# Banded attention and a gated MLP on one core: the next pair's queries are scaled behind the scores of the pair at hand

## The chip, the cores and the metric

One core of one Trainium2 chip. The metric is the device time of one execution in microseconds (us); smaller is better. The times shown are from repeated executions of the whole program; one further execution was taken with the hardware profiler, and everything said of single instructions comes from that one. TensorE is called PE below, VectorE DVE, ScalarE ACT, GpSimd POOL; SP is the engine that issues the DMAs.

## What is computed

Attention over 4 batches of 8 heads (768 positions, 64 numbers a head), where a position sees the first 8 positions and the last 96, with a distance penalty per head; the heads' outputs side by side are the input of an MLP with the gate h * clip(h + 3, 0, 6) / 6.

```
scores = q @ k.T / sqrt(D) - slope[h] * dist      # kept where global or local, else -1e9
a = exp(scores - max); a = a / (sum(a) + 1e-9)
x = (a @ v) for all heads, as [B * S, H * D]      # [3072, 512]
h = x @ w_in                                      # [3072, 2048]
out = (h * clip(h + 3, 0, 6) / 6) @ w_out         # [3072, 512]
```

## The kernel before, in words

The 3072 rows are cut into 8 **blocks** of 384 rows (half a batch each). Of each block, attention is done in 4 **pairs** of heads, numbered through from 0 to 31; pair n belongs to block n // 4. A block's MLP runs in 16 steps f: `first` (L174) makes 128 of the 2048 hidden columns from the four pairs' outputs `xh`, `xl` in 12 matmuls, `gate` (L185 on ACT, L186 on DVE) makes `g`, `high` (L192, on POOL after the first blocks) and `rest` (L199, on DVE) split it in `gh` and `gl`, and `second` (L206) adds 9 matmuls to three accumulators.

Attention of one block is laid between the MLP steps of the block before it. The first nine pairs (0 to 8) are done another way, ahead of 150 us in the profile. Pairs 9 to 31 go through these steps:

- `scale` (L850, POOL): multiplies the queries of a pair in place, in the tile they were loaded into. The scores read them afterwards.
- `packed`: the scores, 24 small matmuls (L864, PE; the trace shows 48 records), then the mask and the row minimum (L893, DVE) and the exponentials with their sums (L897, ACT).
- `sum_up` (L907, L908, DVE) and `normalize` (L917, POOL, six instructions a pair, two for each tile t).
- `spread`: six 32x32 block transposes (L939, DVE) into `blocks`, which has one buffer, and behind the last of them four DMAs (L944, SP) to the DRAM tile `there`; then `fetch`, eight DMAs (L955, SP) from `there` into `weights`.
- `values` (L973, PE): weights times v. Its first four multiplications wait for the first four of the eight fetches, the fifth for the other four.

Loads: the keys and queries of pair n + 3 are loaded by `load_next` (L327, SP) into the room that pair n used, as soon as pair n's scores are done; there are three rooms (load_72, load_73, load_74).

What sets the order: `units[k]` is a list of calls that are made at the k-th yield of the generator which writes out the MLP steps (`halves` up to the end of block 1, `twos`, which takes two steps f together, from block 2 on). `in_order` ties the instructions of PE, SP and POOL to the order in which they are written; ACT and DVE are ordered by a scheduler when the program is built. Each engine runs its instructions in its order, so an instruction that waits holds up all behind it on its engine. In `halves`, step f's `first` is followed by one yield, then by `second` of step f - 1, then by another. `rest_of_third` fills the units for pairs 9 to 11 (and scales 12), `attention` those for pairs 12 to 31, four of a block at a time.

Of the kernel before, what the change touches and what calls it, by code (L numbers as in the profile page):

```python
# [20 lines left out]
NT = 3  # L21
# [44 lines left out]
class Kernel:  # L66
# [616 lines left out]
    def rest_of_third(self, x, slices):  # L683

        units = [[] for _ in range(2 * NF)]
        pairs = [Pair(self, n, x, False) for n in range(EARLY, 3 * NPAIR + 1)]
        pairs[0].scale()
        for p, (me, after) in enumerate(zip(pairs, pairs[1:])):
            at = units[3 * p + 1:]
            at[0] += [me.packed, lambda me=me: self.load_next(me.n, False)]  # L690
            at[1] += [me.sum_up] + [lambda t=t, me=me: me.normalize(t) for t in range(NT)]
            at[2] += [lambda t=t, me=me: me.spread(t) for t in range(NT)] + [me.fetch, after.scale]
        units[10].append(lambda: pairs[0].values("x"))
        units[2 * slices - 1].append(lambda: pairs[-3].values("x"))
        return units, pairs

    def attention(self, i, x, first):

        units = [[] for _ in range(2 * NF - 2)]
        pairs = [first]  # L700
        first.x = x
        for p in range(NPAIR):
            n = i * NPAIR + p
            me, after = pairs[p], Pair(self, n + 1, x, False) if n + 1 < len(self.blocks) * NPAIR else None
            pairs.append(after)
            at = units[6 * p:]
            at[0] += [me.packed, lambda me=me: self.load_next(me.n, False)]
            at[3] += [me.sum_up, lambda me=me: me.normalize(0), lambda me=me: me.normalize(1)]
            at[4] += [lambda me=me: me.normalize(2), lambda me=me: me.spread(0)]
            at[5] += [lambda me=me: me.spread(1), lambda me=me: me.spread(2), me.fetch]  # L710
            if after:
                at[4].append(after.scale)
            if p % 2 == 1:
                at[11] += [lambda me=pairs[p - 1]: me.values("x"), lambda me=me: me.values("s")]
        return units, pairs[NPAIR]
# [336 lines left out]
```

## Time and profile before

| what | us |
|---|---|
| three executions | 664.86, 662.81, 660.73 |
| their median | 662.81 |
| the profiled execution | 660.4 |
| its span, first to last instruction | 658.5 |
| PE busy in it | 640.4 |

The profiled execution took 1.9 us more than its span and lies 2.4 us below the median of the three. In the profile a row of the timeline gives the start in us from the span's start, the duration, the engine, the line, the operation, the tiles out<-in, the shapes, the count, and in brackets the idle time of the engine just before it and what ended that. A row with x48 joins 48 records. A queue's rows (SPq) show the time that the issue of a DMA takes, not its transfer.

### The profile page before, as it was taken

Reading aid. Unit: us, or ns where it says so; the run is one execution under the profiler, and the core shown is the slowest. Engines: PE = TensorE matmul, PEld = TensorE weight load, DVE = VectorE, ACT = ScalarE, POOL = GpSimd, SP = SyncE. Lnnn points to the kernel's source line nnn. Section 1 sums busy time; section 2 is a strip of 40 time slices with the busy share of each in tenths; the row PEclk is TensorE's granted clock in tenths of the full one; section 3 lists DMA queues with packets and bytes.
Section 4 is the critical chain, followed back from the end, with each engine's and each line's share of the span. In section 5 each row is a group of like instructions: output and inputs, shape, how many; then the busy total and the mean of one; then the engine's idle time right before and its main releaser. Section 6 shows DMA issues by size and latency. Waiting matters only on the chain.

```text
span 658.5 us, 13101 instructions
## 1 busy us (share of the span) xinstructions
PE 640.4 (97%) x4761; PEld 565.3 (86%) x4761; DVE 357.2 (54%) x1066; ACT 257.2 (39%) x706; POOL 166.8 (25%) x372
## 2 busy tenths in 40 slices
PE   9989999999799899999999999999999999999997
PEld 7778999997688788988898888988899888989985
DVE  5889999995544554255444454345552555422222
ACT  5897777775324232134313322132321433121111
POOL 4666000001431322033231243113230232202100
PEclk9999999999999999999999999999999999999999
DMA  7675545433564465326552365424653354300001
GB/s 275 183 231 198 193 151 159 136 122 113 134 189 156 122 166 166 96 83 161 173 158 76 115 173 167 125 92 132 179 144 93 102 143 121 103 30 21 1 0 54
DMA packets 47122, 86.23 MB, mean 131 GB/s; under 512 B 6504, under 2 KB 28872, under 8 KB 47048
## 3 DMA queue, kind: packets, MB, share of 16 engines
q1 hardware_dynamic: 46760, 85.03, 43.6%
q8 instruction: 40, 0.66, 0.4%
q14 instruction: 34, 0.28, 0.1%
q10 hardware_dynamic: 288, 0.26, 0.1%
HBM read 60.30 MB, written 24.97 MB: 129 GB/s over the span
## 4 chain that ended last, share of the span: by engine, by line
PE 87%; DVE 5%; ACT 3%; POOL 3%; issue 1%; DMA 1%; SPq 0%; POOLq 0%; ACTq 0%; DVEq 0%
PE hp L174 40%; PE acc L206 35%; PE xp L973 2%; ACT n L897 2%; PE sp L864 2%; PE sp L973 2%; POOL n L917 2%; PE sp L206 1%; PE xp L206 1%; PE tp L206 1%; DVE n L893 1%; DMA load<-pairs 1%; DVE blocks L939 1%; PE tp L864 1%; PE acc L973 1%
## 5 line engine op out<-in xcount | busy, mean ns | idle before, releaser
L185 ACT ACTIVATE g<-hp,small 128x384 f32<-128x384 f32 x127 | 73.5, 579 | 280.2 <-PE hp L174 187.0
L174 PE MATMUL hp<-xh,w1h 128*128 128x384 f32 x512 | 173.9, 340 | 0.5 <-ACT w1h L461 0.5
L174 PE MATMUL hp<-xh,w1l 128*128 128x384 f32 x512 | 172.4, 337 | 0.5 <-DVE w1l L450 0.5
L174 PE MATMUL hp<-xl,w1h 128*128 128x384 f32 x512 | 171.7, 335 | 0.0
L186 DVE SCALAR_TENSOR_TENSOR g<-g,hp 128x384 f32<-128x384 f32 x128 | 70.7, 553 | 128.0 <-ACT g L185 126.8
L192 POOL TENSOR_SCALAR gh<-g 128x384 fp32r<-128x384 f32 x104 | 53.3, 512 | 342.4 <-DVE g L186 316.3
L206 PE MATMUL acc<-w2h,gh 128*128 128x512 f32 x336 | 133.2, 397 | 0.0
L206 PE MATMUL acc<-w2h,gl 128*128 128x512 f32 x336 | 131.8, 392 | 0.0
L206 PE MATMUL acc<-w2l,gh 128*128 128x512 f32 x336 | 131.6, 392 | 0.0
L199 DVE TENSOR_TENSOR gl<-g,gh 128x384 fp32r<-128x384 f32 x128 | 71.5, 558 | 71.7 <-POOL gh L192 58.7
L897 ACT ACTIVATE n<-n,least 128x136 f32<-128x136 f32 (+2 forms) x192 | 79.5, 415 | 70.3 <-DVE least L893 69.5
L174 PEld LDWEIGHTS hp<-xh,w1h 128*128 128x128 f32 x512 | 96.1, 188 | 6.5 <-issue 3.1
L174 PEld LDWEIGHTS hp<-xl,w1h 128*128 128x128 f32 x512 | 96.1, 188 | 2.5
L174 PEld LDWEIGHTS hp<-xh,w1l 128*128 128x128 f32 x512 | 96.1, 188 | 1.1 <-DVE w1l L450 0.8
L917 POOL TENSOR_SCALAR n<-n,sums 128x136 f32<-128x136 f32 (+2 forms) x186 | 81.5, 455 | 45.9 <-DVE sums L908 27.2
L206 PEld LDWEIGHTS acc<-w2h,gh 128*128 128x128 f32 x336 | 63.1, 188 | 15.3 <-issue 3.1
L206 PEld LDWEIGHTS acc<-w2h,gl 128*128 128x128 f32 x336 | 63.0, 188 | 13.8 <-DVE gl L199 0.3
L206 PEld LDWEIGHTS acc<-w2l,gh 128*128 128x128 f32 x336 | 63.1, 188 | 11.5
L939 DVE STREAM_TRANSPOSE blocks<-n 128x256 f32<-128x256 f32 x138 | 51.0, 423 | 23.3 <-POOL n L917 22.7
L897 ACT ACTIVATION_READ_ACCUMULATOR n<-n,least 128x1 f32 x192 | 36.0, 187 | 0.0
L893 DVE CUSTOM_DVE_ANT_0 n<-sp,dl 128x136 f32<-128x136 f32 x60 | 17.7, 295 | 16.1 <-PE tp L864 16.1
L410 ACT ACTIVATE wz<-wst 128x512 f32<-128x512 f32 x32 | 21.4, 673 | 6.2 <-DVE w2l L450 2.8
(119 smaller groups left out, 647.3 us busy)
## 6 DMA issues: line engine op xcount, KB each, us to landing
there<-blocks SPq DMA_DIRECT2D x92, 192.0 KB
wst<-w SPq DMA_DIRECT2D x32, 512.0 KB
weights<-there SPq DMA_DIRECT2D x161, 96.0 KB
load<-pairs SPq DMA_DIRECT2D x31, 444.0 KB
load<-pairs SPq DMA_DIRECT2D x32, 384.0 KB
out<-o SPq DMA_DIRECT2D x23, 256.0 KB
weights<-there SPq DMA_DIRECT2D x23, 24.0 KB
there<-blocks SPq DMA_DIRECT2D x4, 72.0 KB
```

The source lines that it names most:

```text
L174: self.nc.tensor.matmul(hp, lhsT=self.w1(w, f)[:, kt, :], rhs=a[:, kt, :], start=(n == 0), stop=(n == 3 * NKT - 1))
L185: nc.scalar.activation(out=g, in_=hp, func=AF.Relu, bias=self.three, scale=1.0)
L186: nc.vector.scalar_tensor_tensor(out=g, in0=g, scalar=6.0, in1=hp, op0=ALU.min, op1=ALU.mult)
L192: self.nc.gpsimd.tensor_scalar(out=gh, in0=g, scalar1=1.0, scalar2=0.0, op0=ALU.mult, op1=ALU.add)
L199: self.nc.vector.tensor_tensor(out=gl, in0=g, in1=gh.bitcast(F32), op=ALU.subtract)
L206: self.nc.tensor.matmul(acc[tt], lhsT=a[:, tk], rhs=self.w2(w, f), start=(f == 0 and j == 0), stop=(f == NF - 1 and j == 2))
L410: self.nc.scalar.activation(out=self.z[i].bitcast(F32), in_=words[:, :, 1].bitcast(F32), func=AF.Abs)
L893: nc.vector.tensor_tensor_reduce(out=e[:, j, lo:end], in0=sp[j][:, lo:end], in1=d, op0=ALU.add, op1=ALU.min, scale=scale, scalar=3.0e38, a ...
L897: nc.scalar.activation(out=e[:, j, lo:end], in_=e[:, j, lo:end], func=AF.Exp, bias=self.least[:, i:i + 1], scale=-1.0, accum_out=self.sums ...
L917: nc.gpsimd.tensor_scalar(out=e[:, j, lo:end], in0=e[:, j, lo:end], scalar1=over, scalar2=0.0, op0=ALU.mult, op1=ALU.add)
L939: nc.vector.transpose(out=self.blocks[:, :, s, t].rearrange("p b j q -> p j b q"), in_=e[:, :, c:c + P].rearrange("p j (b q) -> p j b q", ...
L973: nc.tensor.matmul(xps[j * D:(j + 1) * D, t * P:(t + 1) * P], lhsT=vt[0:K, t, j * D:(j + 1) * D], rhs=self.part(t, j, c, K), start=(c == 0 ...
```

## The change

The call that scales the queries of pair n + 1 is moved from behind the normalization (and, for pairs 10 to 12, behind the transposes) of pair n to right behind the call that makes pair n's scores. Nothing is added or removed: 23 scalings before and after.

```
--- before.py
+++ after.py
@@ -687,9 +687,9 @@
-            at[0] += [me.packed, lambda me=me: self.load_next(me.n, False)]
+            at[0] += [me.packed, after.scale, lambda me=me: self.load_next(me.n, False)]
             at[1] += [me.sum_up] + [lambda t=t, me=me: me.normalize(t) for t in range(NT)]
-            at[2] += [lambda t=t, me=me: me.spread(t) for t in range(NT)] + [me.fetch, after.scale]
+            at[2] += [lambda t=t, me=me: me.spread(t) for t in range(NT)] + [me.fetch]
@@ -704,12 +704,10 @@
-            at[0] += [me.packed, lambda me=me: self.load_next(me.n, False)]
+            at[0] += [me.packed] + [a.scale for a in (after,) if a] + [lambda me=me: self.load_next(me.n, False)]
             at[3] += [me.sum_up, lambda me=me: me.normalize(0), lambda me=me: me.normalize(1)]
             at[4] += [lambda me=me: me.normalize(2), lambda me=me: me.spread(0)]
             at[5] += [lambda me=me: me.spread(1), lambda me=me: me.spread(2), me.fetch]
-            if after:
-                at[4].append(after.scale)
```

The changed file is two lines shorter, so lines below the change have numbers that are smaller by two (L850 is L848 there, L917 is L915, L939 is L937, L893 is L891).

First place: POOL, from the scaling of pair 9 (load_72) to the normalization of pair 11. The rooms go round, so load_73 is pair 10, load_74 pair 11, the second load_72 pair 12. Before:

```order
L850 TENSOR_SCALAR load_72<-load_72,over 128x384
L192 TENSOR_SCALAR gh<-g 128x384 x2
L917 TENSOR_SCALAR n<-n,sums 128x136 x6
L850 TENSOR_SCALAR load_73<-load_73,over 128x384
L192 TENSOR_SCALAR gh<-g 128x384
L917 TENSOR_SCALAR n<-n,sums 128x136 x6
L192 TENSOR_SCALAR gh<-g 128x384
L850 TENSOR_SCALAR load_74<-load_74,over 128x384
L192 TENSOR_SCALAR gh<-g 128x384
L917 TENSOR_SCALAR n<-n,sums 128x136 x6
L850 TENSOR_SCALAR load_72<-load_72,over 128x384
```

And of the change, on the same engine and from the same place:

```order
L848 TENSOR_SCALAR load_72<-load_72,over 128x384
L192 TENSOR_SCALAR gh<-g 128x384
L848 TENSOR_SCALAR load_73<-load_73,over 128x384
L192 TENSOR_SCALAR gh<-g 128x384
L915 TENSOR_SCALAR n<-n,sums 128x136 x6
L192 TENSOR_SCALAR gh<-g 128x384
L848 TENSOR_SCALAR load_74<-load_74,over 128x384
L915 TENSOR_SCALAR n<-n,sums 128x136 x6
L192 TENSOR_SCALAR gh<-g 128x384
L848 TENSOR_SCALAR load_72<-load_72,over 128x384
```

Each scaling stands ahead of the six normalizations that it stood behind, and pair 11's (load_74) ahead of one `gh` as well.

Second place: POOL, the first two pairs of block 3, 12 and 13, in `attention`; load_73 is pair 13 here, load_74 pair 14. Before:

```order
L192 TENSOR_SCALAR gh<-g 128x384 x5
L917 TENSOR_SCALAR n<-n,sums 128x136 x4
L192 TENSOR_SCALAR gh<-g 128x384 x2
L917 TENSOR_SCALAR n<-n,sums 128x136 x2
L850 TENSOR_SCALAR load_73<-load_73,over 128x384
L192 TENSOR_SCALAR gh<-g 128x384 x2
L917 TENSOR_SCALAR n<-n,sums 128x136 x6
L850 TENSOR_SCALAR load_74<-load_74,over 128x384
```

Of the change:

```order
L848 TENSOR_SCALAR load_73<-load_73,over 128x384
L915 TENSOR_SCALAR n<-n,sums 128x136 x4
L192 TENSOR_SCALAR gh<-g 128x384 x2
L915 TENSOR_SCALAR n<-n,sums 128x136 x2
L848 TENSOR_SCALAR load_74<-load_74,over 128x384
L192 TENSOR_SCALAR gh<-g 128x384 x2
L915 TENSOR_SCALAR n<-n,sums 128x136 x6
```

Pair 13's scaling is ahead of all six normalizations of pair 12 and of two `gh`; pair 14's stands ahead of pair 13's normalization and two `gh`.

Third place: DVE, which the scheduler orders, behind the scores of pair 10. Before:

```order
L907 TENSOR_SCALAR sums<-sums 128x6
L908 RECIPROCAL sums<-sums 128x6
L939 STREAM_TRANSPOSE blocks<-n 128x2x4x32 x6
L186 SCALAR_TENSOR_TENSOR g<-g,hp 128x384
L199 TENSOR_TENSOR gl<-g,gh 128x384
```

Of the change:

```order
L199 TENSOR_TENSOR gl<-g,gh 128x384
L905 TENSOR_SCALAR sums<-sums 128x6
L906 RECIPROCAL sums<-sums 128x6
L937 STREAM_TRANSPOSE blocks<-n 128x2x4x32 x2
L186 SCALAR_TENSOR_TENSOR g<-g,hp 128x384
L937 STREAM_TRANSPOSE blocks<-n 128x2x4x32 x4
L199 TENSOR_TENSOR gl<-g,gh 128x384
```

Here the `gl` that stood ahead of pair 10's six L893 now stands behind them, and the next step's `g` (L186) has moved in between the transposes. From there to the end of the banded part DVE's order is the same; PE, SP and ACT have the same order throughout it.

## The prediction

> **What bounds the kernel now.** I read the profile's page first (busy shares and PE's granted clock), then the list of PE's waits, then the timelines of PE, POOL, DVE and SP around those waits.
>
> ```profile
> PE 640.4 (97%) x4761; PEld 565.3 (86%) x4761; DVE 357.2 (54%) x1066; ACT 257.2 (39%) x706; POOL 166.8 (25%) x372
> PEclk9999999999999999999999999999999999999999
> ```
>
> PE is the bound, at full clock in every slice. It is idle for 658.5 - 640.4 = 18.1 us, and no change that leaves its instructions alone can bring more than that. Which part of it hangs on the scaling, PE's waits tell:
>
> ```profile
> PE acc L864 <- POOL load L850: 3.1, 1, 3.1
> PE sp L864 <- POOL load L850: 2.3, 2, 2.0
> PE acc L864 <- DVE g L186: 1.2, 1, 1.2
> ```
>
> The scores (L864) wait three times for the scaling, 5.4 us in all, and once, 1.2 us, for something put down to DVE. The places:
>
> ```profile
> 166.75 0.58 POOL L850 TENSOR_SCALAR load<-load,over 128x384 f32<-128x384 f32 x1
> 167.38 1.04 PE L864 MATMUL acc<-load 64*32 64x136 f32 x48 [1.24 <-DVE g L186]
> 171.98 2.15 POOL L917 TENSOR_SCALAR n<-n,sums 128x136 f32<-128x136 f32 x6 [3.96 <-DVE sums L908]
> 176.97 0.99 POOL L850 TENSOR_SCALAR load<-load,over 128x384 f32<-128x384 f32 x1
> 178.01 1.04 PE L864 MATMUL acc<-load 64*32 64x136 f32 x48 [3.11 <-POOL load L850]
> 217.38 0.58 POOL L850 TENSOR_SCALAR load<-load,over 128x384 f32<-128x384 f32 x1
> 218.01 0.30 PE L864 MATMUL sp<-load 64*32 64x136 f32 x1 [2.03 <-POOL load L850]
> 370.40 0.58 POOL L850 TENSOR_SCALAR load<-load,over 128x384 f32<-128x384 f32 x1
> 371.04 0.30 PE L864 MATMUL sp<-load 64*32 64x136 f32 x1 [0.28 <-POOL load L850]
> ```
>
> Each time PE starts 0.05 to 0.06 after the scaling ends (167.33, 177.96, 217.96, 370.98): these are pairs 10, 11, 13 and 21. At pair 10 the row names DVE's L186, but the scaling ends at the same moment, and the scores have no operand from L186; I count it to the scaling. The scaling is late because POOL runs in order and has it behind the six normalizations, which wait for the exponentials of the pair before (3.96 us at 171.98).
>
> **The change part by part.** *Removed: the four waits.* Between instructions that wait for nothing the next one starts a little ahead of the modelled end of the last:
>
> ```profile
> 200.55 0.40 PE L206 MATMUL xp<-w2h,gl 128*128 128x512 f32 x1
> 200.88 1.32 PE L973 MATMUL acc<-weights,load 128*64 128x128 f32 x20
> ```
>
> 200.95 against 200.88: 0.07. So a wait that goes is worth its idle time and 0.07: 1.31 (pair 10), 3.18 (pair 11), 2.10 (pair 13), 0.35 (pair 21), together 6.94 us. In the new order pair 10's scaling follows the `gh` of 157.99 and pair 11's that of 167.51:
>
> ```profile
> 174.51 0.40 PE L206 MATMUL xp<-w2h,gl 128*128 128x512 f32 x1
> 157.99 0.51 POOL L192 TENSOR_SCALAR gh<-g 128x384 fp32r<-128x384 f32 x1 [5.53 <-DVE g L186]
> 167.51 0.51 POOL L192 TENSOR_SCALAR gh<-g 128x384 fp32r<-128x384 f32 x1 [0.18 <-DVE g L186]
> 208.43 0.51 POOL L192 TENSOR_SCALAR gh<-g 128x384 fp32r<-128x384 f32 x1 [2.03 <-DVE g L186]
> ```
>
> They end near 159.1 and 168.6. PE wants pair 10's at 167.38 - 1.31 = 166.1 and pair 11's behind the row of 174.51, at 174.91 - 0.07 - 1.31 = 173.5. Pair 13's follows the `gh` of 208.43 and ends at 209.5, wanted at 215.9. All are early by 4.9 us or more, and pair 21's at the like place of its block too, so the waits go whole.
>
> *What is late next.* PE now reaches the values (L973) of pair 11, the last work of block 1, 1.31 + 3.18 = 4.49 earlier: at 200.88 - 4.49 = 196.4. They need the fetched weights of pair 11, which come by SP:
>
> ```profile
> 168.05 3.24 SPq L944 DMA_DIRECT2D there<-blocks  x4
> 173.82 3.58 SPq L955 DMA_DIRECT2D weights<-there  x8
> 177.52 0.36 SPq L327 DMA_DIRECT2D load<-pairs  x1
> 177.98 2.34 SPq L944 DMA_DIRECT2D there<-blocks  x4
> 183.45 4.24 SPq L955 DMA_DIRECT2D weights<-there  x8
> 187.80 0.35 SPq L327 DMA_DIRECT2D load<-pairs  x1
> 188.25 2.25 SPq L944 DMA_DIRECT2D there<-blocks  x4
> 193.72 3.54 SPq L955 DMA_DIRECT2D weights<-there  x8
> 167.26 0.76 DVE L939 STREAM_TRANSPOSE blocks<-n 128x256 f32<-128x256 f32 x2
> ```
>
> From 168.05 to 197.26 SP runs one chain for pairs 9, 10 and 11: four writes, the wait until they have landed, eight reads, one load, and at once the next pair's writes. Pair 10's writes start 0.1 after the load's issue, pair 11's too, so this chain waits for DMAs alone and not for the compute that gets earlier. Its head, 168.05, hangs on pair 9's transposes (the last ends at 168.02), ahead of the first wait that goes, and in the same place in the new order. So pair 11's last fetch is issued at 196.8 as before. When does it land? The DMA view of 193 to 200 us, in 40 slices of 0.175 us:
>
> ```profile
> GB/s 35 0 0 0 0 0 0 0 0 48 167 277 154 202 250 123 233 228 88 263 237 162 277 180 158 272 189 263 255 49 105 193 158 158 281 351 439 334 158 140
> ```
>
> The writes to DRAM end in the first slice (193.2), and SP, which waits for them, issues at 193.72: about 0.5 from the last byte to the one who waits. The fetches run from slice 10 and ebb in slice 30, at 198.2; the rest is the two loads behind them. So the second half of the weights is there for PE at 198.2 + 0.5 = 198.7. The values' first four of ten multiplications need only the first half and can go before; the fifth began 4/10 of the way through the row of 1.25 us (200.88 to 202.13), at 201.4, and now begins at 198.7: the gain up to there is 2.7 at best, and 200.88 - 198.7 = 2.2 if all ten wait. I take 2.5, nearer to what the two separate waits of the program allow. Of the 4.49 us, 2.0 are given back in a new wait at the values of pair 11.
>
> The Trainium skill, DMA: Bandwidth & Descriptors, section Anatomy of one DMA (told there of DMAs that GpSimd issues), puts a fixed cost of about 2.0 us on a transfer and most of it behind the last byte. As an estimate by that page the weights would be usable only near 199.3, 2 us behind the last issue, and the gain up to there would be about 2.1 instead of 2.5. The row of this trace, 0.5 behind the last byte, does not agree, and the sum goes by the row.
>
> *Moved on DVE*, behind pair 10's scores:
>
> ```profile
> 168.05 0.56 DVE L199 TENSOR_TENSOR gl<-g,gh 128x384 fp32r<-128x384 f32 x1
> 173.81 2.08 DVE L939 STREAM_TRANSPOSE blocks<-n 128x256 f32<-128x256 f32 x6 [2.00 <-POOL n L917]
> 175.81 0.52 DVE L186 SCALAR_TENSOR_TENSOR g<-g,hp 128x384 f32<-128x384 f32 x1
> 172.66 0.39 PE L206 MATMUL sp<-w2h,gh 128*128 128x512 f32 x1
> L850 POOL TENSOR_SCALAR load<-load,over x23: 578/582/986, 151.9 to 549.8; 128x384 f32<-128x384 f32 x23
> ```
>
> `gl` stands behind six L893 (0.30 each by a row below, 1.8 at most) and ends by 170.4 instead of 168.6; PE's `second` that reads it begins at 172.66 - 1.31 = 171.35. `g` follows two transposes (0.7) instead of six and ends near 175.1; its `gl`, behind the other four, ends near 177.1, just when PE's third matmul of that `second` wants it. That is a few tenths at most, and they fall in the 2.0 us that pair 11's values wait anyway; if that cover is gone they cost 0.2.
>
> *Moved on POOL.* 0.58 us (0.99 once) now stands ahead of a normalization or `gh`. POOL is busy a quarter of the time and waits for sums or `g` at those places (2.03 to 5.53 us in the rows above), so nothing is charged; were each passed on whole, 0.6 a pair would sit in the fetch chains, which have to spare what the next rows say.
>
> *Pair 13.* Its wait gone, PE comes to the values of pair 13 earlier by 2.5 + 2.1 = 4.6. The chain there:
>
> ```profile
> 217.43 0.77 DVE L939 STREAM_TRANSPOSE blocks<-n 128x256 f32<-128x256 f32 x2 [0.56 <-POOL n L917]
> 219.03 0.30 DVE L893 CUSTOM_DVE_ANT_0 n<-sp,dl 128x136 f32<-128x136 f32 x1 [0.83 <-PE tp L864]
> 235.11 3.55 SPq L955 DMA_DIRECT2D weights<-there  x8
> 242.36 0.83 PE L973 MATMUL sp<-weights,load 128*64 128x128 f32 x12
> ```
>
> Pair 13's L893 can start when the transposes are through (218.2, which shifts by 2.5), 3.3 earlier, and the fetch with it: issued by 235.4, and with the 1.4 that pair 11's took from the end of issue to use, there at 236.8. PE wants it at 242.36 - 4.6 = 237.8. It holds, with 1 us to spare, and the 2.1 stay.
>
> **Sum.** 2.5 + 2.1 + 0.35 = 4.95, say 5.0 us: 660.4 - 5.0 = 655.4 for an execution like the profiled one. The median of the runs shown lies 2.4 above that execution; with the same distance the forecast is 657.8. It is 0.75% less, and about 1% is what a measurement of this kernel can tell from no change.
>
> **Rivals.** (1) *The whole 6.9 us come through*: pair 11's fetch gets earlier too, or PE does not have to wait for all of it. For it: three of four waits sit before that chain's last part. Against: the chain's gapless SP rows. It gives 653.5 by the profile, 655.9 as a median. (2) *Pair 13 gives its 2.1 back*: if its fetch stayed where it is, issued by 238.7 and there at 240.1, PE would wait 2.3 us at its values. For it: it follows pair 12's on one queue, as in block 2. Against: pair 12's transposes follow PE's steps and move with them. Gain 2.9: 659.9. (3) *The change does not do what it says*: the scores wait for another thing that ends just when the scaling did (the L186 row is the hint), gain 1 or less: 662. For it only that row; against it the other three rows. (4) *Slower*: the scaling now stands in POOL's order ahead of the normalization, and it waits for its own load. If a load lands after POOL gets there, normalization, fetch and `gh` all wait behind it. The nearest case:
>
> ```profile
> 159.86 0.45 SPq L327 DMA_DIRECT2D load<-pairs  x1
> ```
>
> This is pair 12's load; by the 5.5 us from issue to landing of the writes (188.25 to 193.72) it is there at 165.4, and POOL gets to it behind the `gh` of the `g` that ends at 175.1, near 175.7. It decides from loads 10 us later than now; beyond that each us can cost one at each of the ten places in blocks 3 to 7 where PE makes the values of two pairs, so 1 us too late loses 10 and leaves 5 more than before: 668.
>
> **How the numbers follow.** Chances: forecast 0.70, (1) 0.12, (2) 0.08, (3) 0.05, (4) 0.05. The range takes the forecast, (1) and (2), with medians of 655.9 to 659.9, and half of the scatter of the three runs (4.1 us) at each end: 653.8 to 662.0. Faster by over 1% (below 656.2) is more than half of (1) and a sixth of the forecast, whose median would have to come out 1.6 low: 0.18. Slower by over 1% is (4): 0.04. The rest, 0.78, is within 1%.
>
> **What would show it.** Right: in PE's waits no row L864 <- L850; a new row of PE at L973 of about 2 us, near 197 to 199, ended by a DMA; SP's eight rows at the same times within 0.3; block 1's end earlier by 2.5, pair 13's scores by 4.6, everything from pair 21 on by 5.0; POOL's busy time the same. Wrong: L973 of pair 11 without a wait (rival 1), a wait at L973 near 238 (2), the four waits of L864 with another name (3), idle time on POOL ahead of L848 put down to a DMA (4).

## The result, and the profile after

| | before | changed |
|---|---|---|
| median of the runs, us | 662.16 (6 runs, 659.45 to 664.86) | 654.88 (6 runs, 654.59 to 656.52) |
| ratio | | 0.9898, 95% interval 0.987 to 0.9927 |
| profiled execution, us | 660.4 | 654.68 |
| its span, us | 658.5 | 652.9 |

The change makes the kernel faster by 1.0%, 6.8 us by the ratio. The forecast was 657.8, a gain of 5.0; the range of 653.8 to 662.0 holds the time. The two profiles differ by 5.6 us in span, of which 0.3 lies ahead of pair 9, where nothing was changed (its scores start at 158.64 and 158.33). One run of the first experiment below took 1048 us at a granted clock of 0.557 over the whole program and is left out of its figures.

The list of PE's waits, changed kernel:

```profile
PE xp L971 <- DVE xl L161: 2.1, 4, 1.0
PE xp L971 <- issue: 1.4, 1, 1.4
PE tp L923 <- ACT pt L927: 1.0, 1, 1.0
PE acc L971 <- DMA weights<-there: 1.0, 1, 1.0
```

All three rows of the scores (L864, now L862) are gone; the fourth row is new, PE waiting for fetched weights. The timeline of PE shows where, and DVE's and POOL's show why:

```profile
165.76 0.96 PE L862 MATMUL acc<-load 64*32 64x136 f32 x48
173.11 0.96 PE L862 MATMUL acc<-load 64*32 64x136 f32 x48
196.65 0.66 PE L971 MATMUL acc<-weights,load 128*64 128x128 f32 x8
198.31 0.88 PE L971 MATMUL acc<-weights,load 104*64 104x128 f32 x12 [1.00 <-DMA weights<-there]
212.86 0.30 PE L862 MATMUL sp<-load 64*32 64x136 f32 x1
166.49 0.56 DVE L186 SCALAR_TENSOR_TENSOR g<-g,hp 128x384 f32<-128x384 f32 x1
158.16 0.99 POOL L848 TENSOR_SCALAR load<-load,over 128x384 f32<-128x384 f32 x1
167.69 0.60 POOL L848 TENSOR_SCALAR load<-load,over 128x384 f32<-128x384 f32 x1
205.90 0.59 POOL L848 TENSOR_SCALAR load<-load,over 128x384 f32<-128x384 f32 x1
```

The scores of pairs 10, 11 and 13 have no bracket any more: their scalings end 6.6, 4.8 and 6.4 us ahead. Pair 10's scores start while the L186 to which the wait of before was put down is still to come (166.49), so that wait was the scaling's. The values of pair 11 now run in two pieces, eight records with the first half of the weights and, 1.00 us of idleness later, twelve with the second.

SP's rows of the same chain as before, changed kernel:

```profile
167.75 2.10 SPq L942 DMA_DIRECT2D there<-blocks  x4
172.54 3.59 SPq L953 DMA_DIRECT2D weights<-there  x8
176.24 0.36 SPq L327 DMA_DIRECT2D load<-pairs  x1
176.70 2.46 SPq L942 DMA_DIRECT2D there<-blocks  x4
183.33 3.55 SPq L953 DMA_DIRECT2D weights<-there  x8
186.99 0.35 SPq L327 DMA_DIRECT2D load<-pairs  x1
187.43 2.18 SPq L942 DMA_DIRECT2D there<-blocks  x4
192.89 3.54 SPq L953 DMA_DIRECT2D weights<-there  x8
```

It starts where it did (168.05, less the 0.3 of the start), is as gapless, and ends 0.83 earlier, 0.5 without the offset, where the prediction had it at the same times within 0.3.

### The profile page after: what moved, and what is told of

It reads as the page before. It is cut to its first block, busy times and chain, and to the rows that moved or that the text cites. A ratio compares the mean times of both kernels' runs of the same rounds, so it can differ in the third digit from the quotient of the medians.

```text
span 652.9 us, 13102 instructions
## 1 busy us (share of the span) xinstructions
PE 639.4 (98%) x4761; PEld 564.1 (86%) x4761; DVE 356.9 (55%) x1066; ACT 257.4 (39%) x706; POOL 167.6 (26%) x372
## 4 chain that ended last, share of the span: by engine, by line
PE 83%; DVE 6%; ACT 4%; DMA 2%; POOL 2%; issue 2%; SPq 1%; POOLq 0%; ACTq 0%
PE hp L174 38%; PE acc L206 35%; ACT n L895 3%; PE xp L971 3%; PE sp L862 2%; PE sp L971 2%; DMA there<-blocks 1%; POOL n L915 1%; SPq L953 1%; DVE n L891 1%; PE xp L206 1%; PE tp L206 1%; PE sp L206 1%; DVE blocks L937 1%; DVE wz L453 1%
## 5 line engine op out<-in xcount | busy, mean ns | idle before, releaser
L186 DVE SCALAR_TENSOR_TENSOR g<-g,hp 128x384 f32<-128x384 f32 x128 | 70.7, 553 | 123.3 <-ACT g L185 122.1
L915 POOL TENSOR_SCALAR n<-n,sums 128x136 f32<-128x136 f32 (+2 forms) x186 | 81.8, 457 | 38.3 <-DVE sums L906 23.1
L937 DVE STREAM_TRANSPOSE blocks<-n 128x256 f32<-128x256 f32 x138 | 51.1, 423 | 25.3 <-POOL n L915 20.8
L891 DVE CUSTOM_DVE_ANT_0 n<-sp,dl 128x136 f32<-128x136 f32 x60 | 17.7, 295 | 14.7 <-PE tp L862 14.7
```

The costliest lines, as they stand in the source:

```text
L186: nc.vector.scalar_tensor_tensor(out=g, in0=g, scalar=6.0, in1=hp, op0=ALU.min, op1=ALU.mult)
L891: nc.vector.tensor_tensor_reduce(out=e[:, j, lo:end], in0=sp[j][:, lo:end], in1=d, op0=ALU.add, op1=ALU.min, scale=scale, scalar=3.0e38, a ...
L915: nc.gpsimd.tensor_scalar(out=e[:, j, lo:end], in0=e[:, j, lo:end], scalar1=over, scalar2=0.0, op0=ALU.mult, op1=ALU.add)
L937: nc.vector.transpose(out=self.blocks[:, :, s, t].rearrange("p b j q -> p j b q"), in_=e[:, :, c:c + P].rearrange("p j (b q) -> p j b q", ...
```

## The experiments

Eight runs: six other kernels, and the kernel before and the changed one once more. The expectations count them in the order in which they were put on record: their first experiment is the sixth here, their fourth the third. Where the pieces start in each profile (pair 9's scores are untouched by all and give each profile's offset):

| profile | pair 9 | 10 | 11 | values 11 | 12 | 13 | 14 | 21 | span |
|---|---|---|---|---|---|---|---|---|---|
| before | 158.64 | 167.38 | 178.01 | 200.88 | 206.51 | 218.01 | 231.60 | 371.04 | 658.5 |
| changed | 158.33 | 165.76 | 173.11 | 196.65 | 203.48 | 212.86 | 226.43 | 365.63 | 652.9 |
| pairs 10 to 12 only | 158.17 | 165.60 | 172.95 | 196.60 | 203.45 | 214.95 | 230.09 | 369.22 | 656.8 |
| pairs 13 to 31 only | 157.69 | 166.43 | 176.86 | 201.26 | 206.89 | 216.30 | 229.89 | 368.90 | 656.4 |
| loads behind the fetch | 158.16 | 165.59 | 172.94 | 195.74 | 201.37 | 210.78 | 224.37 | 363.38 | 651.1 |
| scaling three times | 158.77 | 166.18 | 173.53 | 196.59 | 203.60 | 212.98 | 226.55 | 365.50 | 653.1 |
| before again | 158.22 | 166.96 | 177.09 | 199.94 | 205.56 | 217.07 | 232.18 | 371.60 | 659.2 |
| before, waits filled | 158.26 | 167.01 | 176.78 | 199.65 | 205.28 | 216.78 | 230.35 | 369.70 | 657.6 |
| changed again | 158.21 | 165.65 | 173.00 | 197.35 | 206.09 | 215.47 | 229.04 | 367.99 | 655.2 |
| all loads behind | 158.18 | 165.61 | 172.96 | 195.75 | 201.38 | 210.76 | 224.33 | 363.28 | 650.7 |

**1. The first half of the change alone.** Edit, on the kernel before:

```
-            at[0] += [me.packed, lambda me=me: self.load_next(me.n, False)]
+            at[0] += [me.packed, after.scale, lambda me=me: self.load_next(me.n, False)]
...
-            ... + [me.fetch, after.scale]
+            ... + [me.fetch]
```

> Only the first half of the change: the scaling of pairs 10 to 12 moved, that of 13 to 31 as before. Theory: the waits of pairs 10 and 11 go, the wait of about 1 us at the values of pair 11 comes, and the wait of 2.03 at pair 13 stays: the start of block 2 is 2.6 us earlier than before, and so is the end; ratio 0.996. Rival (the two halves hang together, pair 13's wait being a late echo of pairs 10 and 11): pair 13's wait goes or shrinks by more than 1 us, and the end is 4 us earlier or more.

Ratio 0.9944 (0.9918 to 0.997), median of nine runs 658.2. Pairs 10 and 11 start as in the changed kernel. Its list of PE's waits has the new one for the weights, and pair 13's still:

```profile
PE sp L864 <- POOL load L850: 2.0, 1, 2.0
PE acc L973 <- DMA weights<-there: 1.3, 2, 1.0
```

Pair 13 starts 3.06 earlier than before, 2.6 without the offset. So the wait at pair 13 has its own cause, and the halves add.

**2. The second half alone.** Edit, on the changed kernel:

```
-            at[0] += [me.packed, after.scale, lambda me=me: self.load_next(me.n, False)]
+            at[0] += [me.packed, lambda me=me: self.load_next(me.n, False)]
...
-            ... + [me.fetch]
+            ... + [me.fetch, after.scale]
```

> Only the second half: the scaling of pairs 13 to 31 moved, that of 10 to 12 as before. Theory: waits at pairs 10 and 11 as before (1.24 and 3.11), no wait for the weights at the values of pair 11, no wait at pairs 13 and 21: the end 2.5 us earlier (2.10 + 0.35 and a few hundredths at pairs 17, 25 and 29); ratio 0.996. Rival: pair 13's values then wait for their weights and the 2.1 come back; the end within 1 us of before.

Ratio 0.9954 (0.9928 to 0.9979), median 658.1. The list of PE's waits has those of pairs 11 and 10 and none for weights:

```profile
PE acc L862 <- POOL load L848: 2.9, 1, 2.9
PE acc L862 <- DVE g L186: 1.2, 1, 1.2
```

From pair 12 to 13 it takes 9.41 where before took 11.50, so 2.09 of the forecast's 2.10. Pair 13's values do not give them back.

**3. Two loads moved out of the fetch chain.** Edit, on the changed kernel, in `rest_of_third`:

```
-            at[0] += [me.packed, after.scale, lambda me=me: self.load_next(me.n, False)]
+            at[0] += [me.packed, after.scale] + [lambda me=me: self.load_next(me.n, False)] * (p == 0)
...
+        units[9] += [lambda n=n: self.load_next(n, False) for n in (EARLY + 1, EARLY + 2)]
```

> The whole change, and the loads of the keys and queries of pairs 13 and 14 issued behind the fetch of pair 11 instead of between the transfers of pairs 9, 10 and 11. Theory (what was given back hangs on SP's chain for the pairs 9 to 11): without the two issues (0.45 us each) and without their 444 KB beside the writes, the fetch of pair 11 lands 1 to 3 us earlier, PE does not wait at the values of pair 11 nor at the gl ahead of them, and reaches block 2 by 1.0 to 1.9 us earlier than the change alone: ratio to before 0.987. Rival (the chain's length is the writes' and reads' own latency, and the loads do not matter): the fetch lands at the same time within 0.9 us and the wait of about 1 us at the values of pair 11 stays.

Ratio 0.9866 (0.9822 to 0.9911), 652.55 to 653.5 in four runs, all below the changed kernel's lowest of 654.59. Its SP and PE rows:

```profile
176.05 2.04 SPq L943 DMA_DIRECT2D there<-blocks  x4
180.80 3.64 SPq L954 DMA_DIRECT2D weights<-there  x8
184.54 2.19 SPq L943 DMA_DIRECT2D there<-blocks  x4
189.33 3.54 SPq L954 DMA_DIRECT2D weights<-there  x8
195.74 1.32 PE L972 MATMUL acc<-weights,load 128*64 128x128 f32 x20
```

Pair 11's fetch begins 3.6 earlier, the values run in one piece without a wait, and pair 12 starts 2.1 earlier than in the changed kernel (1.9 without the offset). The loads cost the chain more than their issue: in the eight profiles with a load right ahead of them, the writes of pairs 10 and 11 took 5.45 to 6.63 us from issue to the fetch, and 4.75 and 4.79 here without. The rival falls.

**4. The scaling three times over.** Edit, on the changed kernel, in `scale`:

```
+        for _ in range(2):
+            nc.gpsimd.tensor_scalar(out=q, in0=q, scalar1=1.0, scalar2=0.0, op0=ALU.mult, op1=ALU.add)
```

> The whole change, with every scaling followed by two more instructions of the same size on POOL that multiply the queries by 1: 1.2 us more on POOL at each of the 23 places. Theory (POOL has slack there, so a moved scaling costs nothing): the span within 0.6 us of the change's own 652.9, no new wait of PE at the scores, the wait at the values of pair 11 within 0.5 us of its 1.0; ratio to before 0.990. Rival (the 0.6 us of each scaling sit in the chain of normalization, transposes and fetch, uncovered): with 1.2 us more a pair, PE waits at the values of the two pairs, ten times up to 1.2 us, and the span grows by 3 us or more.

Ratio 0.9908 (0.9879 to 0.9936), median 655.5, span 653.1 against 652.9, and one wait alone near the change:

```profile
PE acc L973 <- DMA weights<-there: 1.2, 1, 1.2
```

POOL's time at the new place is free, even 1.2 us more of it.

**5. All loads behind the fetch.** Edit, on the third experiment's kernel, in `attention`:

```
-            at[0] += ... + [lambda me=me: self.load_next(me.n, False)]
+            at[0] += ...
...
-            at[5] += [..., me.fetch]
+            at[5] += [..., me.fetch, lambda me=me: self.load_next(me.n, False)]
```

> As the fourth experiment (pairs 13 and 14 loaded behind pair 11's fetch), and in blocks 3 to 7 too each load of keys and queries is issued behind its pair's fetch, some 13 us later than in the change. Theory: PE's steps do not move, since the loads are still there when POOL reaches the scaling, or late by less than the fetch chain's slack of 1 us: the span within 0.5 us of the fourth experiment's 651.1. Rival (the prediction's slower case: the scaling, first in POOL's order, waits for its load, and normalization and fetch behind it): POOL idles ahead of the scaling for a DMA, PE waits at the values of two pairs, and the span grows by 1 us or more.

Ratio 0.9868 (0.984 to 0.9895), 652.5 to 653.32, span 650.7. It reaches the point from which the prediction's slower case decides, at pair 16's scaling:

```profile
237.09 0.59 POOL L849 TENSOR_SCALAR load<-load,over 128x384 f32<-128x384 f32 x1 [0.26 <-DMA load<-pairs]
```

POOL waits 0.26 us for a load there, and PE loses nothing by it. That load is issued 11 us later than in the changed kernel (233.07 against 223.91, with pair 13 2.1 earlier). The slower case exists as a mechanism, but only loads later than that would bring it about.

**6. The kernel before, again.** No edit.

> The kernel before, unchanged, for a second profile and for the granted clock of each run. Theory A: the four waits of the scores for the scaling are a matter of the program's order and come back at the same places with the same lengths (1.24 at pair 10, 3.11 at pair 11, 2.03 at pair 13, 0.28 at pair 21, each within 0.2); the ratio is 1.000 within 0.003, and the part of the measured gain (6.8 us by the ratio) that the two profiles do not show (5.3 us from pair 10 on) goes with the granted clock of the runs. Rival B: the waits differ from execution to execution; then this profile has other lengths, by 1 us or more in sum.

Ratio 1.000 (0.9971 to 1.0028), 658.89 to 663.94 in ten runs. The waits come back at the same places (1.2, 2.6, 2.0 and 0.3), pair 11's 0.5 shorter, more than the 0.2 that was allowed for. Two rows ahead of it show on what it hangs:

```profile
172.89 2.08 DVE L939 STREAM_TRANSPOSE blocks<-n 128x256 f32<-128x256 f32 x6 [1.50 <-DMA there<-blocks]
175.56 0.51 POOL L192 TENSOR_SCALAR gh<-g 128x384 fp32r<-128x384 f32 x1 [1.86 <-DVE g L186]
```

Pair 10's transposes wait until pair 9's four writes have left the one buffer `blocks`; the next `g` stands behind them on DVE, and pair 11's scaling behind the `gh` of that `g` on POOL. SP issues pair 9's fetch when the same writes have landed, and in all four profiles with before's order at this place pair 11's scores start 4.18 or 4.19 us behind that issue. So the length of pair 11's wait varies with a DMA. (The first profile puts the wait of these transposes down to POOL, but they start at 173.81, with SP's fetch at 173.82.)

The clock does not agree between the two profiles either. The view by windows (length, busy time of PE, PEld, which is PE's loading of weights, DVE, ACT and POOL, then the granted clock, DMA share and GB/s) for the stretch behind pair 13's wait, in the first profile of before:

```profile
217.00:221.00 4.00, 2.99 (x60) 2.78 (x61) 2.18 (x14) 1.57 (x8) 0.96 (x3) 1.00 0.47 98
```

and in this one:

```profile
217.00:221.00 4.00, 3.93 (x57) 3.53 (x58) 1.66 (x13) 1.96 (x10) 0.01 (x1) 0.57 0.70 154
```

Two matmuls there, in PE's timeline of the first profile:

```profile
219.37 0.35 PE L174 MATMUL hp<-xh,w1l 128*128 128x384 f32 x1
219.55 0.34 PE L174 MATMUL hp<-xh,w1h 128*128 128x384 f32 x1
```

and of this one, with the wait ahead of them:

```profile
217.07 0.30 PE L864 MATMUL sp<-load 64*32 64x136 f32 x1 [2.03 <-POOL load L850]
219.34 0.52 PE L174 MATMUL hp<-xh,w1l 128*128 128x384 f32 x1
219.66 0.52 PE L174 MATMUL hp<-xh,w1h 128*128 128x384 f32 x1
```

Behind the same wait of 2.03 us the matmuls follow each other by 0.32 instead of 0.18, and the clock over the four microseconds is 0.57: 3.4 us at one half (4 x 0.43 / 0.5). From pair 13 to pair 14 that is 15.11 instead of 13.59, a loss of 1.52. The same happened behind pair 13's wait in the first experiment and behind pair 11's in the second.

The granted clocks of the runs say it too. Of the 52 runs of the kernel before in these experiments, 16 have a clock of 0.999 or more and average 659.5 us, 14 have 0.996 or 0.997 and average 660.9, 12 have 0.994 and average 662.5, and 10 have 0.991 or 0.992 and average 664.2. As an estimate from the 3.4 us above, one stretch at half clock takes 0.0026 off the clock of the whole program, so these are runs with about none, one, two and three of them.

**7. The waits of before filled with idle work.** Edit, on the kernel before, in `packed` ahead of the scores:

```
+        for _ in range({11: 10, 13: 8}.get(self.n, 0)):
+            nc.tensor.matmul(banks[0][:, 0, 0:P], lhsT=kk.ident, rhs=kk.ident, start=True, stop=True)
```

> The kernel before, its order unchanged, with matmuls of no use laid in PE's two longest waits: 10 ahead of the scores of pair 11 and 8 ahead of those of pair 13 (0.234 us each by the same shape at the start of the program, so 2.3 and 1.9 us), into the bank that the scores overwrite. Theory (a wait of PE of 2 to 3 us costs more than its length in some executions, since the clock then stands at one half for 3.41 us, as the profile of the first experiment shows behind pair 13's wait): no such window behind pairs 11 and 13, the profiled span within 0.5 us of 658.5, the runs within 2.5 us of each other instead of 6, and their median 1.0 to 2.0 us below before's: ratio 0.997. Rival (the runs of before scatter for another reason): median and scatter as before's, ratio 1.000 or a little more.

Ratio 0.9972 (0.9955 to 0.9989), and twelve runs between 659.09 and 660.47, where seventeen of before on the same chip lie between 658.58 and 664.77. PE's timeline has the filling and what is left of pair 13's wait:

```profile
174.36 2.39 PE L860 MATMUL acc<-ident 128*128 128x128 f32 x20
214.57 1.95 PE L860 MATMUL sp<-ident 128*128 128x128 f32 x16
216.78 0.30 PE L866 MATMUL sp<-load 64*32 64x136 f32 x1 [0.26 <-POOL load L850]
```

and the window behind it the full clock:

```profile
217.00:221.00 4.00, 4.00 (x67) 3.79 (x52) 1.67 (x14) 2.80 (x13) 0.00 (x0) 1.00 0.80 193
```

The kernel is faster by 1.9 us by the ratio and its scatter is gone: all its runs have a clock of 0.998 or more, and their median of 659.47 is what the runs of before at full clock average. PE does matmuls of no use and keeps its clock. This is the part of the waits' cost that no sum over one profile held. (In this one profile pair 13's scores also start earlier, by 0.85 less the offset than in the first profile of before and by 0.33 than in the second, and the span is 0.9 below the first's where at most 0.5 was expected. Pair 11's are as much earlier, by 0.85 and 0.35: pair 9's writes, which lie ahead of the filling, landed sooner.)

**8. The changed kernel, again.** No edit.

> The changed kernel once more, for a second profile and its runs on the same chip. Theory: no wait of the scores, one wait of 1.0 within 0.3 at the values of pair 11, the pairs' scores within 0.5 us of the first profile once the start is taken off; no window of half clock except at the end; ratio 0.990. Rival: the profile has other waits, or a window of half clock behind the wait of 1.0.

Ratio 0.9898 (0.987 to 0.9925), three runs at 654.76 to 655.02 and the profiled one at 657.01. It shows that the change has left one place of this kind. PE's timeline at the values of pair 11:

```profile
197.35 0.66 PE L971 MATMUL acc<-weights,load 128*64 128x128 f32 x8 [1.03 <-DMA weights<-there]
199.33 0.88 PE L971 MATMUL acc<-weights,load 104*64 104x128 f32 x12 [1.31 <-DMA weights<-there]
```

and the window behind it:

```profile
200.00:204.00 4.00, 4.00 (x17) 3.87 (x14) 0.56 (x1) 0.48 (x1) 0.00 (x0) 0.57 1.00 355
```

Here pair 11's fetch began 0.8 later than in the first profile, PE idled 2.3 us within 3.0, and the half clock followed. My theory of one steady wait of 1.0 was wrong: it varies, and the third experiment, which removes it, is better also because its four runs lie within 1 us.

## Why the prediction was right, and where it was off

*The four waits go*: right. From one pair's scores to the next it takes 1.31 less at pair 10, 3.28 at pair 11, 2.12 at pair 13 and 0.34 at pair 21 (13.51 instead of 13.85), where 1.31, 3.18, 2.10 and 0.35 were forecast. *Pair 10's wait is the scaling's, not DVE's*: shown by the L186 of 166.49. But why pair 11's scaling was late is only half told by the normalizations that the prediction names. They were through at 174.13; then, in before,

```profile
176.49 0.51 POOL L192 TENSOR_SCALAR gh<-g 128x384 fp32r<-128x384 f32 x1 [2.36 <-DVE g L186]
```

a `gh` ahead of the scaling waited 2.36 us more, in the end for pair 9's writes (sixth experiment). The change cures both, since the scaling now stands ahead of both.

*Part is given back at the values of pair 11, on a fetch whose chain does not move*: right in place and kind. Less the offset, 1.9 of the 4.6 us that pair 11's scores had gained are gone at pair 12's; the forecast was 2.0 of 4.49. The row of the wait itself has 1.00 us and not about 2, since PE had lost 0.7 us by the start of the values. From pair 9 to the second piece of the values the profiles differ by 2.75 (198.31 - 158.33 against 201.37 - 158.64), and pair 12's scores gained 2.7; the forecast was 2.5. That it came so close is in part luck: two of its pieces were off and cancelled. The last byte is not 0.5 ahead of its reader but about 0.9: the fetch traffic of the changed kernel ebbs at 197.4 by the DMA view of 192 to 199 us (31st of 40 slices),

```profile
GB/s 105 70 0 0 0 0 0 0 0 0 22 132 259 207 162 281 171 211 237 105 206 277 119 290 193 167 281 193 211 290 62 123 70 88 123 211 281 334 263 439
```

and PE begins at 198.31, 1.9 us behind the end of the last issue (192.89 + 3.54). The 0.5 was SP's wait for writes to DRAM, taken over to PE's wait for reads. The Trainium skill's 2.0 us (DMA: Bandwidth & Descriptors, Anatomy of one DMA), which I set aside, fits these 1.9 better than my row did, though only 0.9 of them lie behind the last byte, where the Trainium skill puts most of its figure. Against that the chain was 0.5 shorter without the offset: from issue to fetch pair 9's writes took 4.79 instead of 5.77 and pair 10's 6.63 instead of 5.47, and the issue of pair 10's fetch took 3.55 instead of 4.24.

*DVE's new order costs a few tenths under cover*: at the steps named no `gl` was late. PE waited 0.18 us for one later, and DVE's row ahead of it names another cause:

```profile
183.43 1.43 DVE L937 STREAM_TRANSPOSE blocks<-n 128x256 f32<-128x256 f32 x4 [2.82 <-DMA there<-blocks]
186.94 0.50 PE L206 MATMUL sp<-w2h,gl 128*128 128x512 f32 x1 [0.18 <-DVE gl L199]
```

Pair 11's transposes wait for pair 10's writes to leave `blocks`, and `g` and `gl` stand behind them. In the third experiment both waits are gone, so this is the DMA chain by another way; it vanished in the wait for the weights. *POOL's time is free*: shown by the fourth experiment. *Pair 13 keeps its 2.1*: shown by the second.

Sum by the profiles: forecast 5.0, measured 5.6 with the offset of 0.3, so 5.3. *The step that failed is the last one of the sum*, "with the same distance the forecast is 657.8". The distance of 2.4 between the median and the profiled execution was taken for a constant of the runs; it was a cost of the waits themselves. The profiled execution happened to have no half clock behind its waits; most others had it at one place or more (of the 52 runs counted in the sixth experiment, 36 have a clock of 0.997 or less). The changed kernel's median lies 0.2 above its profiled execution. The term that was missing measured 1.9 us (seventh experiment), and with it 4.9 of the 6.8 us by the ratio are left for the waits' own length. The runs with a clock of 0.999 or more agree: 659.5 us before, 654.8 in seven runs of the changed kernel, 4.7 apart. So the gain came out at just over 1%, to which the prediction gave 0.18.

## What to carry to other kernels

An instruction that does not depend on its predecessors should not stand behind them in an in-order queue: here 0.6 us of work, moved past a wait, was worth 1%. When a wait goes, look at once for the next thing that PE will reach, and whether its chain gets earlier too; here a DMA chain hardly did, and taking two loads out of it brought 2 us more. And where runs scatter by more than the profile explains, compare the granted clock of several profiles: a gap of PE may cost more than its length.

## What the runs showed of the hardware that was not expected

Four profiles have single waits of PE of 2.0 us or more behind 150 us: before (3.11 and 2.03), before again (2.6 and 2.03) and the two halves (2.03; 2.9). In three of the four one of these waits was followed by 3.4 us at half clock, which cost 1.5 us; in the first profile none was. The changed kernel's second profile has it behind two gaps of 1.03 and 1.31 close together; the profiles whose gaps there are smaller do not have it.

The traces show what tells these cases apart. They record when the granted clock changes, and in all ten profiles each stretch of full clock lasts a whole multiple of 3.413 us: 62 times that in before again (5.61 to 217.23), 57 times in changed again (5.61 to 200.17), 51 times in the second half alone (4.21 to 178.28). So the clock goes by windows of 3.413 us, and they lie elsewhere in each execution. In before again, the window ahead of the half clock and the one at half clock:

```profile
213.82:217.23 3.41, 1.38 (x18) 0.84 (x24) 1.86 (x4) 0.23 (x1) 2.19 (x4) 1.00 0.01 2
217.23:220.64 3.41, 3.41 (x55) 3.00 (x43) 1.43 (x13) 1.60 (x9) 0.00 (x0) 0.50 0.76 166
```

PE is busy for 1.38 us of the first: the whole wait of 2.03 lies in it. In the first profile of before a boundary, 217.51, falls into the same wait:

```profile
214.10:217.51 3.41, 1.89 (x9) 1.23 (x7) 1.41 (x4) 0.58 (x1) 1.74 (x4) 1.00 0.01 2
217.51:220.92 3.41, 2.91 (x59) 2.70 (x60) 2.10 (x14) 1.49 (x7) 0.45 (x1) 1.00 0.55 115
```

The two windows have 1.53 and 0.50 us of idle time, and the clock stays full; pair 11's wait of 3.11 is cut there into 1.65 and 1.46. In all ten profiles, from the start of full clock up to the last 8 us, the windows followed by half clock are the four with 2.03, 2.03, 1.99 and 1.91 us of idle time, and no other window has more than 1.80 (before again, 172.86 to 176.27). So it depends on where the windows happen to lie, and the limit here is between 1.80 and 1.91 us in one window. This is read out of the ten profiles afterwards; no run shifts a wait against the windows to test it.

The Trainium skill, TensorE: Matmul & The Clock Gate, Part 1, tells of such a gate with an idle window of about 3.4 us and says that the window runs free; the length and the change from execution to execution agree, but here 1.91 us of idle time within a window were enough. What sets the start of the windows in an execution was not settled.
